# A fused convolution and two-layer MLP: another order of the first loads, taps without a detour, and wider VectorE calls

## The chip, the cores and the metric

The kernel runs on one core of one Trainium2 chip. The metric is the device time of one execution in microseconds. It is given as the median of several runs; the profile comes from one profiled execution.

## The reference

The input x has 8 sequences of 4096 tokens with 192 features, in float32. Eight heads of 24 features each have seven weights. A causal depthwise convolution comes first, and a two-layer MLP with exact GELU follows.

```python
w = exp(weight - max(weight)); w = w / (sum(w) + 1e-9)      # softmax over the 7 taps of a head
a[b, s, h, :] = sum_k w[h, k] * x_pad[b, s + k, h, :]        # 6 zeros ahead of each sequence
out = gelu(a.reshape(32768, 192) @ w_in) @ w_out             # w_in 192 x 2048, w_out 2048 x 192
```

The output is 32768 x 192 in float32.

## The kernel before

**Layout.** The tokens are cut in two halves of 16384. The two halves lie side by side on the 128 partitions, 64 features of each. The 192 features make three such thirds, `p` = 0, 1, 2 (`NP` = 3). A block `n` takes `WS[n]` tokens of each half: blocks 0 to 5 have 256, all later ones 512.

**Stages of a block.** `load` brings x to `xin` in four DMAs. `trans` (L529) transposes 32x32 squares on VectorE into `xT`. The seven taps follow: one `tensor_scalar` (L555) and six `scalar_tensor_tensor` (L562) for each third, into `acc` and at last `xc` in bf16. `mm1` (L763) multiplies a slice of W_in (`win`) with `xc` into `hp`. ScalarE takes the GELU of the slice into `gT` (L684). `mm2` (L793), or `mm2_t` (L823) for the 512-token blocks, multiplies with W_out and is interleaved with the next block's `mm1`. The results go through `osb` to memory. A slice `(n, i)` is one GELU call; a 256-token block has 8 slices, a 512-token block 16.

**The first two blocks** (`PC`) take their convolution on TensorE. `pconv` (L714) multiplies `xTb`, a bf16 copy of `xT`, with seven diagonal matrices `dg` into PSUM `ob`, and `conv_out` (L191, L193) copies the result to `xc`. Each third is a "kind" in a bank of its own; the last third is cut in two kinds of 128 tokens. The second half kind of the last third is computed crosswise (`ex` = 1), so that it can run in other quadrants of the array beside another kind. Block 0 is loaded in an order of its own: 8 neighbouring tokens in one partition, as runs of 5760 bytes that also hold features that are not used. Its history (`halo`) then takes copies on GpSimd (L417).

**The taps' weights.** The softmax runs on 8 partitions (`wsb`, `wex`, `wrc`), and five transposes (L485, L488) spread the result to all 128 partitions as `wcol`.

**W_in and W_out.** GpSimd's queue carries W_in with a cast to bf16, each half of the partitions getting one half of the columns. `FP` cuts that into a quarter, a quarter and a half (`S_WIN[0..2]`). `dup` on VectorE (L505) copies each piece to the other half of the partitions. SyncE loads W_out in four calls, and GpSimd casts it (L460).

**Order.** Everything is written out by hand: each engine has one list of instructions, and semaphores tie the lists together. The lists that matter here are

- SyncE: `wsb`, half of block 0's x, a wait for `S_WIN[0]`, block 1's x, W_out, x of blocks 2 and 3.
- GpSimd: W_in piece 0, the diagonal mask `idb`, W_in pieces 1 and 2, history of block 0, the bf16 copy of block 1, the casts of W_out.
- VectorE: the softmax, `dg`, `trans` of block 0, `conv_out`, `dup(0)`, `dup(1)`, `trans` of block 1, `dup(2)`, `conv_out` of block 1, then blocks 2, 3, ... with the copies out of PSUM at fixed places (`side`).
- ScalarE: half of block 0's x, the exponential, the casts of block 0, its share of `conv_out`, then the GELUs. For blocks 4 to 6 (`K0`) it also takes the first tap (L657).
- TensorE: 16 matmuls on zeros (L698, "warm"), `pconv` of block 0, then per slice `mm1` and a share of the previous block's `mm2`. The `pconv` of block 1 stands behind slices (0,4) and (0,5).

```python
            share = {1: [4, 12, 8, 8, 8, 8, 8, 8]}     # units of block 0's mm2 behind block 1's slices
                    wait_pc(t, n, NP - 2)              # mm1 of blocks 0, 1: xc's first two thirds
```

Of the kernel before, what the change touches and what calls it, by code (L numbers as in the profile page):

```python
# [11 lines left out]
def bass_lightweight_conv__then__act_gelu_exact_kernel(  # L12
# [16 lines left out]
    TB = 512  # L29
# [23 lines left out]
    HL = 32 * HB  # L53
    XB = HL + WS[0]
# [32 lines left out]
    CH = [[(8 * hf + i) % NF for i in range(NF)] for hf in range(2)]  # L87
# [3 lines left out]
    for n in range(NB):  # L91
        k = 64 if n == 0 or M0 <= n < M1 else 16 * NG[n] if n < NB - 1 else 32 * NG[n]
        OUTS.append(k * (NG[0] if n == 0 else 1) + (OUTS[n - 2] if n >= 2 else 0))
# [15 lines left out]
    with es:  # L109
        win = sbt("win", [128, NP * F], BF16)  # L110
        wout = sbt("wout", [128, NF * C], BF16)
        wsb = sbt("wsb", [H, KS], F32)
        wmx = sbt("wmx", [H, 1], F32)
        wsm = sbt("wsm", [H, 1], F32)
        wrc = sbt("wrc", [H, 1], F32)
        wex = sbt("wex", [H, KS], F32)
        wnm = sbt("wnm", [32, 32], F32)
        wnt = sbt("wnt", [32, 32], F32)
# [20 lines left out]
        S_XIN = [sem("S_XIN%d" % i) for i in range(NX)]  # L139
        S_OUT = [sem("S_OUT%d" % i) for i in range(2)]  # L140
# [32 lines left out]
        def kinds(n):  # L173
            w = WS[n]
            return [(0, 0, 0, w), (1, 1, 0, w), (2, 0, 0, w // 2), (2, 1, w // 2, w // 2)]


        PIECES = [(0, None), (1, 0), (1, 1), (2, None), (3, 0), (3, 1)]

        PA = (0, 2, 3, 5)  # L180

        def conv_out(e, n, j):
            kd, h = PIECES[j]
            p, ex, c0, w = kinds(n)[kd]
            e.wait_ge(S_PC, 4 * PC[n] + kd + 1)
            ro = slice(0, 128) if h is None else slice(64 * h, 64 * h + 64)
            ri = ro if not ex else slice(64 - 64 * h, 128 - 64 * h)
            dst = xc[n % 2][ro, p * TB + c0 : p * TB + c0 + w]
            src = bank(kd, ri, w)
# [5 lines left out]
        def wait_pc(e, n, p):  # L195

            if n == 0:
                e.wait_ge(S_PCA, (1, 2, 4)[p])
                if p >= 1:
                    e.wait_ge(S_PCE, p)  # L200
            else:
                e.wait_ge(S_PCE, 2 + (1, 3, 6)[p])

        NCV = NP * KS
        FQ = F // 8
        FH = F // 2
        FP = [0, FQ, 2 * FQ, FH]

        WG = [0, 4, 2, 6]

        def cast(e, n, p):
            e.wait_ge(S_TR, NP * n + p + 1)
            e.tensor_copy(
                ap(xTb[PC[n]], p * XB + HX, [[NP * XB, 128], [1, WS[n]]]),
                ap(xT[n % 2], p * XW + HX, [[NP * XW, 128], [1, WS[n]]]),
            ).then_inc(S_CAST[PC[n]])

        def cvd(n):

            return sum(NCV - NP * (m in K0) for m in range(n + 1) if m not in PC)  # L220


        HC = [0]
        for n in range(NB):
            HC.append(HC[n] + (1 + NP if n == 0 else 1))
# [5 lines left out]
        def xin_at(n):  # L231

            return 64 * (n // NX + 1)
# [85 lines left out]
        def load(e, n, qs=(0, 2, 1, 3), sm=None):  # L319
            mb = WS[n] // 32  # L320
            if n >= NX:
                e.wait_ge(S_TR, NP * (n - NX + 1))
            for q in qs:
                off = ((q // 2) * HALF + OFF[n]) * D + DQ * (q % 2)
                if n == 0:

                    dst = [[TB // 32 * DQ, 32], [1, mb * D - DQ]]
                    src = [[mb * D, 32], [1, mb * D - DQ]]
                else:
                    dst = [[TB // 32 * DQ, 32], [DQ, mb], [1, DQ]]  # L330
                    src = [[D, 32], [32 * D, mb], [1, DQ]]
# [4 lines left out]
        def store(e, m):  # L336
            if m < M0:
                for g in range(NG[m]):
                    wait_ev(e, m, g)
                    if m > 0:  # L340

                        e.dma_start(
                            ap(
                                outt,
                                (OFF[m] + 128 * g) * C,
                                [[C, 128], [HALF * C, 2], [1, C]],
                            ),
                            ap(osb[m % 2], g * C, [[8 * C, 128], [4 * C, 2], [1, C]]),
                        ).then_inc(S_OUT[m % 2], 16)
                        continue  # L350
                    mb = WS[m] // 32
                    for q in range(4):

                        e.dma_start(
                            ap(
                                outt,
                                (OFF[m] + 4 * g + q) * C,
                                [[mb * C, 32], [HALF * C, 2], [1, C]],
                            ),
                            ap(  # L360
                                osb[m % 2],
                                32 * q * 8 * C + g * C,
                                [[8 * C, 32], [4 * C, 2], [1, C]],
                            ),
                        ).then_inc(S_OUT[m % 2], 16)
# [18 lines left out]
        def _(g):  # L384
            def win_in(c0, c1, sm):
                for hf in range(2):
# [3 lines left out]
                    ).then_inc(sm, 16)  # L390

            win_in(FP[0], FP[1], S_WIN[0])
# [12 lines left out]
            for i in range(1, 3):  # L405
                win_in(FP[i], FP[i + 1], S_WIN[i])

            def halo(n):
                if n == 0:

                    t = xTb[0]
                    g.memset(
                        ap(t, 0, [[NP * XB, 128], [XB, NP], [32, HB]]), 0.0
                    ).then_inc(S_HALO)
                    for p in range(NP):
                        g.wait_ge(S_TR, p + 1)
# [502 lines left out]
```

## Time and profile before

| | us |
|---|---|
| median of 9 runs (682.05 to 684.11) | 682.68 |
| the profiled execution, device time | 683.04 |
| its span | 681.3 |
| PE (TensorE) busy | 674.8 (99%) |
| DVE (VectorE) busy | 561.8 (82%) |
| ACT (ScalarE) busy | 536.1 (79%) |
| POOL (GpSimd) busy | 38.9 (6%) |

PE is busy for nearly the whole span, so the time is what TensorE has to do, plus what it idles. In the profile a row such as `L763 PE MATMUL hp<-xc,win` names the line of the kernel, the engine, the operation and the tiles. The device time lies 1.74 us above the span. One matmul's record overlaps its neighbours', so the time of a stage is read from the starts of its first rows.

### The profile page before, as it was taken

The numbers are of one execution on the slowest core, as the hardware profiler recorded it, in microseconds if no ns is written. First come the engines' busy times: TensorE is split into PE (matmuls) and PEld (weight loads), VectorE is DVE, ScalarE is ACT, GpSimd is POOL, SyncE is SP. The second block draws the span as 40 slices with busy tenths as digits, with TensorE's granted clock in tenths as the row PEclk, the third lists the DMA queues.
The fourth block names the chain that finished last, engine by engine and source line by source line (L and its number), as shares of the span: only waits on it lengthen the run. The fifth ranks groups of instructions, "written<-read, shape, count | busy, mean of one in ns | idle before, by whom it ended". The sixth has DMA issues, their size and how long they took to land.

```text
span 681.3 us, 27316 instructions
## 1 busy us (share of the span) xinstructions
PE 674.8 (99%) x12576; PEld 410.6 (60%) x12576; DVE 561.8 (82%) x906; ACT 536.1 (79%) x548; POOL 38.9 (6%) x57
## 2 busy tenths in 40 slices
PE   8999999999999999999999999999999999999998
PEld 4899755555555555555555555555555555555557
DVE  6899989888889888898888898888898888988611
ACT  6899988777787777787877788777778777778772
POOL 5126100000000000000000000000000000000000
PEclk9999999999999999999999999999999999999999
DMA  9445333133442243432244322334322444311123
GB/s 224 81 105 130 72 71 75 42 76 95 96 93 56 45 93 94 95 78 49 65 95 94 94 65 46 82 94 96 92 51 49 95 94 96 74 45 26 48 50 94
DMA packets 132994, 54.79 MB, mean 80 GB/s; under 512 B 126480, under 2 KB 132752, under 8 KB 132880
## 3 DMA queue, kind: packets, MB, share of 16 engines
q1 hardware_dynamic: 130960, 51.50, 32.3%
q8 instruction: 98, 1.61, 1.0%
q0 software_dynamic: 1248, 0.79, 0.9%
q10 hardware_dynamic: 672, 0.76, 0.4%
q14 instruction: 16, 0.13, 0.1%
HBM read 28.66 MB, written 25.17 MB: 79 GB/s over the span
## 4 chain that ended last, share of the span: by engine, by line
PE 95%; DMA 2%; DVE 1%; SPq 1%; issue 0%; POOL 0%; POOLq 0%
PE hp L763 47%; PE ob L823 43%; PE ob L793 5%; DMA xin<-in_x_dram 1%; DVE acc L562 1%; PE hp L793 1%; DMA win<-in_moe_w_in_dram 1%; SPq L332 1%; SPq L877 0%; DVE xT L529 0%; POOL win L387 0%; DVE acc L555 0%; DVE xc L562 0%; DVE osb L283 0%; POOLq L904 0%
## 5 line engine op out<-in xcount | busy, mean ns | idle before, releaser
L684 ACT ACTIVATE gT<-hp 128x1024 bf16<-128x1024 f32 x512 | 522.7, 1023 | 129.9 <-PE hp L763 126.6
L763 PE MATMUL hp<-xc,win 64*64 64x512 bf16 (+2 forms) x6048 | 419.3, 366 | 2.4 <-ACT gT L684 1.1
L823 PE MATMUL ob<-gT,wout 64*64 64x512 bf16 x5376 | 366.3, 376 | 0.0
L562 DVE SCALAR_TENSOR_TENSOR acc<-xT,wcol,acc 128x512 f32<-128x512 f32 (+1 forms) x495 | 314.4, 699 | 0.0
L763 PEld LDWEIGHTS hp<-xc,win 64*64 64x64 bf16 (+1 forms) x6048 | 189.9, 106 | 135.2 <-ACT gT L684 3.3
L823 PEld LDWEIGHTS ob<-gT,wout 64*64 64x64 bf16 x5376 | 172.1, 118 | 123.0
L314 DVE STREAM_TRANSPOSE osb<-ob 128x512 f32<-128x512 f32 x84 | 74.2, 886 | 99.8 <-PE ob L823 99.8
L529 DVE STREAM_TRANSPOSE xT<-xin 128x512 f32<-128x512 f32 (+1 forms) x105 | 78.6, 796 | 4.2 <-DMA xin<-in_x_dram 4.2
L562 DVE SCALAR_TENSOR_TENSOR xc<-xT,wcol,acc 128x512 bf16<-128x512 f32 (+1 forms) x99 | 65.1, 712 | 0.0
L450 POOL COPY xT<-xT 128x18 f32<-128x18 f32 x30 | 27.9, 929 | 504.9 <-DVE xT L529 482.6
L793 PE MATMUL ob<-wout,gT 64*128 64x192 bf16 x896 | 47.6, 243 | 0.0
L793 PEld LDWEIGHTS ob<-wout,gT 64*128 64x128 bf16 x896 | 40.1, 94 | 3.9 <-issue 0.4
L555 DVE TENSOR_SCALAR acc<-xT,wcol 128x512 f32<-128x512 f32 (+1 forms) x90 | 37.6, 473 | 1.1
L698 PE MATMUL hp<-warm 128*128 128x512 bf16 x16 | 6.1, 562 | 1.3 <-DVE warm L466 1.3
L285 ACT ACTIVATE osb<-ob 128x192 f32<-128x192 f32 x2 | 0.7, 330 | 7.1 <-PE ob L793 7.1
L793 PE MATMUL hp<-wout,gT 64*128 64x192 bf16 x128 | 5.9, 243 | 0.0
L283 DVE COPY osb<-ob 128x192 f32<-128x192 f32 x2 | 0.7, 358 | 6.1 <-PE ob L793 6.1
L793 PEld LDWEIGHTS hp<-wout,gT 64*128 64x128 bf16 x128 | 5.3, 94 | 0.0
L657 ACT ACTIVATE acc<-xT,wcol 128x256 f32<-128x256 f32 (+1 forms) x9 | 5.2, 575 | 0.0
L698 PEld LDWEIGHTS hp<-warm 128*128 128x128 bf16 x16 | 2.1, 136 | 4.7 <-issue 3.2
L270 ACT ACTIVATE osb<-ob 128x384 f32<-128x384 f32 x10 | 4.9, 486 | 0.0
L387 POOL DMA_DIRECT2D win<-in_moe_w_in_dram x6 | 3.9, 658 | 0.8 <-POOLq L904 0.8
(36 smaller groups left out, 30.7 us busy)
## 6 DMA issues: line engine op xcount, KB each, us to landing
out_dram<-osb SPq DMA_DIRECT2D x122, 192.0 KB, 3.1
xin<-in_x_dram SPq DMA_DIRECT2D x116, 192.0 KB, 4.1
xin<-in_x_dram SPq DMA_DIRECT2D x20, 96.0 KB, 3.7
woutf<-in_moe_w_out_dram SPq DMA_DIRECT2D x4, 384.0 KB, 6.2
win<-in_moe_w_in_dram POOLq DMA_DIRECT2D x4, 96.0 KB, 4.3
win<-in_moe_w_in_dram POOLq DMA_DIRECT2D x2, 192.0 KB, 4.9
out_dram<-osb SPq DMA_DIRECT2D x8, 48.0 KB, 1.9
out_dram<-osb ACTq DMA_DIRECT2D x4, 96.0 KB, 2.0
```

The source lines that it names most:

```text
L314: v.transpose(ap(osb[m % 2], j, [[8 * C, 128], [C // 2, TB // 32], [NP, 32]]), bank(ring(m, j)),).then_inc(S_EV)
L332: e.dma_start(ap(xin[n % NX], 32 * q * (TB // 32 * DQ), dst), ap(xt, off, src)).then_inc(sm or S_XIN[n % NX], 16)
L450: g.tensor_copy(dst, src).then_inc(S_HALO)
L529: v.transpose(ap(xT[n % 2], p * XW + HX, [[NP * XW, 128], [1, w]]), ap(xin[n % NX], p, [[TB // 32 * DQ, 128], [D if n == 0 else DQ, w // 3 ...
L555: ins = v.tensor_scalar(a, src, wk, None, ALU.mult)
L562: ins = v.scalar_tensor_tensor(dst, src, wk, a, op0=ALU.mult, op1=ALU.add)
L657: a.activation(out=acc[n % 2][:, p * TB : p * TB + w], in_=ap(xT[n % 2], p * XW + HX, [[NP * XW, 128], [1, w]]), func=AF.Copy, scale=wcol[ ...
L684: a.activation(out=ap(gT[n % 2], i * c * 2 * w, dst), in_=ap(hp[u % 2], 0, src), func=AF.Gelu,).then_inc(S_GELU)
L698: t.matmul(hp[1][:, 0:512], warm[:, 0:128], warm[:, :])
L763: ins = t.matmul(hp[u % 2][fo : fo + fw, o : o + w], ap(win, f1, [[NP * F, 64], [2, fw]]), xc[n % 2][r, p * TB : p * TB + w], start=(p == ...
L793: ins = t.matmul(bb[sub], gT[m % 2][r, c0 : c0 + 128], wout[r, CH[sub][i] * C : (CH[sub][i] + 1) * C], start=(ph == 0 and i == 0), stop=(p ...
L823: ins = t.matmul(bank(ring(m, j), slice(64 * h, 64 * h + 64), w), ap(wout, 64 * hf * NF * C + CH[h][i] * C + j, [[NF * C, 64], [NP, 64]],) ...
```

## The change

Seven edits are made together:

1. Block 0's x is loaded like every other block's, in runs of 384 bytes. Its history is a memset on VectorE, and GpSimd's copies for it go.
2. GpSimd's queue carries, after the mask, the first half of each W_in half, then block 1's x (with its own semaphore `S_XP`), then the second half. `dup` has two steps and `CH` another order of the column chunks, so that slices (0,0), (0,1) need the first half, (0,2), (0,3) its copy, (0,4), (0,5) the second half and (0,6), (0,7) its copy. W_out comes in another grouping to match, and `UO` orders block 0's `mm2`.
3. SyncE waits for `S_WIN[1]` before W_out, and loads x of block 2 ahead of W_out's last part.
4. The softmax runs on all 128 partitions; two DMAs bring the weights there. The five transposes go.
5. The last third of block 0 is computed straight in both of its kinds, and `conv_out` copies it in two calls in place of three. `mm1` of slice (0,0) takes the last third after both chunks of the others.
6. Taps come in two calls (two thirds, one third) in place of three, `trans` in one call from block 2 on; the places in `side` are counted anew. `mm1` of a block waits for two thirds first.
7. Ten warm matmuls in place of 16; `pconv` of block 1 begins behind slice (0,3); `share` changes.

```diff
-    CH = [[(8 * hf + i) % NF for i in range(NF)] for hf in range(2)]
+    CH = [[(8 * hf + 8 * (i // 4 % 2) + 4 * (i // 8) + i % 4) % NF for i in range(NF)] for hf in range(2)]
...
-        PA = (0, 2, 3, 5)
+        PA = (0, 2, 3)
+        PV = (1, 4)
...
-        FP = [0, FQ, 2 * FQ, FH]
+        FP = [0, FH // 2, FH]
...
-                if n == 0:
-                    dst = [[TB // 32 * DQ, 32], [1, mb * D - DQ]]
-                    src = [[mb * D, 32], [1, mb * D - DQ]]
-                else:
-                    dst = [[TB // 32 * DQ, 32], [DQ, mb], [1, DQ]]
-                    src = [[D, 32], [32 * D, mb], [1, DQ]]
+                dst = [[TB // 32 * DQ, 32], [DQ, mb], [1, DQ]]
+                src = [[D, 32], [32 * D, mb], [1, DQ]]
...
-            win_in(FP[0], FP[1], S_WIN[0])
             g.wait_ge(S_MSET, 1)
...
-            for i in range(1, 3):
-                win_in(FP[i], FP[i + 1], S_WIN[i])
+            win_in(FP[0], FP[1], [S_WIN[0]] * 2)
+            load(g, 1, sm=S_XP)
+            win_in(FP[1], FP[2], S_WIN[1:])
...
-            halo(0)
             halo(1)
             for p in range(NP):
                 cast(g, 1, p)
-            for i in range(4):
+            halo(2)
+            for k in range(4):
...
-            v.memset(wnm[:, :], 0.0).then_inc(S_MSET)
-            v.wait_ge(S_WSB, 16)
+            v.memset(ap(xTb[0], HF, [[NP * XB, 128], [XB, NP], [1, HB]]), 0.0).then_inc(S_HALO)
+            v.wait_ge(S_WSB, 32)
...
-            v.transpose(wnt[:, :], wnm[:, :]).then_inc(S_PRO)
-            v.wait_ge(S_PRO, 5)
-            for q in range(4):
-                v.transpose(
-                    wcol[32 * q : 32 * q + 32, :],
-                    ap(wnt, 4 * (q % 2), [[32, 32], [1, 4], [0, 8]]),
-                ).then_inc(S_PRO)
...
-                ops = [] if n in K0 else [("t", n, p) for p in range(NP)]
-                ops += [("c", n, k, p) for k in range(int(n in K0), KS) for p in range(NP)]
+                ops = [] if n in K0 else [("t", n, 0)]
+                ops += [("c", n, k, q) for k in range(int(n in K0), KS) for q in range(2)]
                 if n + 1 in K0:
-                    ops[9:9] = [("t", n + 1, p) for p in range(NP)]
+                    ops[6:6] = [("t", n + 1, 0)]
...
             dup(0)
-            dup(1)
             for p in range(NP):
                 trans(1, p)
-            dup(2)
+            dup(1)
...
-                for j, at in enumerate([(n + 2, 18), (n + 3, 6), (n + 3, 9)]):
+                for j, at in enumerate([(n + 2, 12), (n + 3, 4), (n + 3, 6)]):
...
-            for i in range(16):
+            for i in range(10):
                 t.matmul(hp[1][:, 0:512], warm[:, 0:128], warm[:, :])
...
-            order = [0] * 4 + [1, 0] * 3 + [1, 2] * 4 + [3, 2] * 3 + [3] * 4
-            for kd in order:
+            for kd in [0] * 4 + [1, 0] * 3 + [1, 2, 2] * 3 + [1, 2] + [3] * 7:
                 pconv(*seq[kd].pop(0))
...
-                (0, 4): [(1, kd, k) for k in taps for kd in (0, 1)],
+                (0, 3): [(1, kd, k) for k in taps if k > 3 for kd in (0, 1)],
+                (0, 4): [(1, kd, k) for k in taps if k <= 3 for kd in (0, 1)],
...
-                        t.wait_ge(S_CV, cvd(n))
+                        t.wait_ge(S_CV, cvd(n) - 1)
...
-            share = {1: [4, 12, 8, 8, 8, 8, 8, 8]}
+            share = {1: [4, 4, 4, 10, 10, 10, 11, 11]}
...
-            sp.wait_ge(S_WIN[0], 32)
-            load(sp, 1)
-            for i in range(4):
-                g = WG[i]
-                sp.dma_start(
-                    ap(woutf, 2 * g * C, [[NF * C, 128], [2 * C, 2], [1, 2 * C]]),
-                    ap(woutt, 256 * g * C, [[2 * C, 128], [256 * C, 2], [1, 2 * C]]),
-                ).then_inc(S_WOUT[i], 16)
+            def wout_in(k):
+                sp.dma_start(
+                    ap(woutf, 2 * k * C, [[NF * C, 128], [8 * C, 2], [1, 2 * C]]),
+                    ap(woutt, 256 * k * C, [[2 * C, 128], [1024 * C, 2], [1, 2 * C]]),
+                ).then_inc(S_WOUT[k], 16)
+
+            sp.wait_ge(S_WIN[1], 16)
+            for k in range(3):
+                wout_in(k)
             load(sp, 2)
+            wout_in(3)
             load(sp, 3)
```

## The prediction

> **What bounds the kernel now.** I read the page first, then the stretches of time, the chain of waits, and the timeline of the first 30 us. The stretches (span, busy us of PE, PEld, DVE, ACT and POOL with counts, granted clock, DMA share, GB/s):
>
> ```profile
> 7.24:9.07 1.83, 1.54 (x57) 1.38 (x57) 0.74 (x3) 1.34 (x5) 0.60 (x3) 1.00 1.10 163
> 9.07:18.23 9.16, 7.75 (x152) 5.16 (x152) 7.20 (x16) 7.52 (x10) 4.01 (x6) 1.00 1.13 283
> 18.23:29.59 11.36, 10.69 (x224) 9.93 (x225) 9.49 (x25) 9.56 (x11) 1.28 (x3) 1.00 0.38 77
> 29.59:71.86 42.27, 42.27 (x898) 42.17 (x900) 42.23 (x90) 37.64 (x49) 16.59 (x4) 1.00 0.45 105
> 71.86:667.78 595.92, 595.92 (x10978) 339.39 (x10976) 495.22 (x754) 474.06 (x466) 11.11 (x27) 1.00 0.31 74
> ```
>
> From 29.59 us, when block 2's `mm1` starts, TensorE has no idle time at all until the last block's end. So the time is the moment of that start plus a fixed rest, unless VectorE falls behind; between 29.59 and 71.86 it is busy 42.23 of 42.27 us. Up to 29.59 TensorE starts late (7.24) and idles 2.37 us. The timeline tells what started when (start, us, engine, line, idle time before and its releaser):
>
> ```profile
> 5.92 0.15 PEld L698 LDWEIGHTS hp<-warm 128*128 128x128 bf16 x1 [0.28 <-issue]
> 6.00 1.34 DVE L529 STREAM_TRANSPOSE xT<-xin 128x256 f32<-128x256 f32 x3 [0.75 <-DMA xin<-in_x_dram]
> 6.29 0.53 PEld L698 LDWEIGHTS hp<-warm 128*128 128x128 bf16 x3 [0.21 <-issue]
> 7.24 1.54 PE L714 MATMUL ob<-xTb,dg 64*64 64x256 bf16 x56
> 9.67 1.27 PE L763 MATMUL hp<-xc,win 64*128 64x256 bf16 x20 [0.20 <-ACT xc L191]
> 10.32 4.92 ACT L684 ACTIVATE gT<-hp 128x1024 bf16<-128x1024 f32 x5 [0.71 <-PE hp L763]
> 18.23 0.83 PE L763 MATMUL hp<-xc,win 64*128 64x256 bf16 x12 [0.45 <-ACT gT L684]
> 20.06 1.34 DVE L529 STREAM_TRANSPOSE xT<-xin 128x256 f32<-128x256 f32 x3 [1.90 <-DMA xin<-in_x_dram]
> 29.59 0.83 PE L763 MATMUL hp<-xc,win 64*128 64x256 bf16 x12 [0.66 <-DVE xc L562]
> ```
>
> Two paths meet at 29.59. One goes from block 0's x (6.00) over `pconv` (7.24) and the first GELU (10.32) through TensorE's own work. The other goes from block 2's x (20.06) through its taps, and ended last by 0.66 us. The chain shows where that x was held up:
>
> ```profile
> 2.08 4.75 DMA win<-in_moe_w_in_dram
> 6.85 0.33 SPq L332
> 12.96 7.08 DMA xin<-in_x_dram
> 20.06 1.36 DVE xT L529 x3
> ```
>
> SyncE waited for W_in's first piece, issued block 1's x and all of W_out, and only then block 2's x, which took 7.08 us to land. So both paths must shorten for the time to fall.
>
> **Block 0's x.** It is 184 KB in each of four DMAs now and 96 KB after. Loads of the new kind, alone on the queues at 32 us, against W_in's, from issue to landing (min/median/max; the first line is x at 32 to 37 us, the second W_in):
>
> ```profile
> DMA to landing us min/median/max: 2.2/2.3/2.4
> DMA to landing us min/median/max: 3.6/4.7/5.1
> ```
>
> ScalarE issues its two at 0.87 and 1.30. SyncE's come one issue later than now, because a second DMA for the tap weights goes ahead (issue to issue 0.43): the last at about 2.12. With 2.3 the data is there at 4.45; with the 4.3 that the slowest of block 0's loads took now, at 6.4. I take 4.5, since W_in, the competitor, starts later too.
>
> The Trainium skill speaks against it: "DMA: Bandwidth & Descriptors", Specifications, wants transfers of at least 512 bytes, below which the engine reads, modifies and writes. By that rule 384-byte runs are slow; if each cost double, the landing would be 2.3 later and, as an estimate, the sum 682.7.
>
> The rows give 0.52 MB on SyncE's queue at 44.6% of 16 engines over 4.7 us (32.3 to 37), 15.5 bytes per ns and engine, and 0.37 MB on ScalarE's with 5760-byte packets at 37.2% over 4 us (1 to 5), also 15.5: a byte costs the same in both. I go by the rows, and the sum stays as below.
>
> **The taps.** The weights land 0.43 later (2.61 for 2.18). Reduce to `wcol` without the transposes took 1.25 (2.18 to 3.43), so 3.86, and `dg` takes 0.62: VectorE is free at 4.5, with the x. ScalarE's second table load shifts to 4.54, still ahead of the casts. `trans` starts at 4.55 for 6.00, `pconv` 1.24 later as now, at 5.8. The history copies that go had been hidden behind the casts; with the memset, block 0's stores are also 2 DMAs for 8 (27.11 to 32.6 on SyncE now), which only brings block 5's x sooner. The mask first and W_in after it costs GpSimd 0.64 (1.95 for 1.31).
>
> **`pconv` and the first GELU.** In units of 256 columns both orders make 14.5, so 1.54 stays. Now the last third of `xc` is out 2.43 after `pconv` starts (9.67); after, ScalarE has three copies (0.383, 0.375, 0.277) and VectorE one of 64x256 and one of 128x128 (0.424, 0.292), so it is out about 2.1 after, at 7.9, and two thirds of slice (0,0) are done by then. W_in's first half is issued at 1.95 and 2.65 and lands by the row above at 6.25 to 7.75, so it is just hidden; each 0.1 beyond costs 0.1. First GELU 8.75 for 10.32.
>
> **From there to block 2.** TensorE's work in this stretch is 7 slices and `pconv` of block 1 (7 x 0.66 + 0.96 + 0.59), then block 1's 8 slices and 64 units (16 x 0.66): 16.7 us. Now it takes 29.59 - 10.32 = 19.27, so it idles 2.6. Of this 0.66 is block 2's wait, and 1.2 came from block 1's x (landed 12.4) with `dup(2)` behind it until 15.83. After, GpSimd issues block 1's x at 3.3 to 5.9 and the second half by 7.2 (0.65 a call); W_in's packets ran from 4.8 to 9.7 beside x, some 2.1 us a half, and 1.7 us for x, put x at 9 and the second half at 10.5 to 11.4. GpSimd's own casts of x come after its DMA issues (done by 7.2), so no one waits for those; its `halo(2)`, now ahead of W_out's casts, waits for `trans` at 11.2, before W_out is there. VectorE then runs `dup(0)` 7.9 to 9.9 (2 x 0.98), `trans` to 11.2, `dup(1)` to 13.2, `conv_out` of block 1 to 15.6. Slice (0,2) needs `dup(0)` just when its GELU buffer comes free (9.8), (0,6) needs `dup(1)` at 14. ScalarE at 0.98 a GELU paces block 0, so some idling stays: with 1.5 for 2.6, block 2 can start at 8.75 + 16.7 + 1.5 = 26.95. Ends: 0.9 and 2.6, so 26.3 to 28.0.
>
> **Block 2's x.** SyncE, with W_out queued behind its wait for `S_WIN[1]`, resumes near 10 for 6.83. Ahead of x stand three W_out parts (their packet records show 123 of 1536 bytes in 0.5 us, so 1.04 for the 256 of a part), so x lands near 17, at worst as now relative to the first W_out issue (8.70 to 20.04), less one part and block 1's x: 10 + 11.3 - 1.0 - 1.7 = 18.6. `trans` in one call and two-call taps: 256 elements took 0.401, 512 took 0.667, so 0.135 is fixed per call; 1.07 a tap for 1.20, and 1.17 for `trans`, 0.72 for the first tap: 8.3 for 9.4, two thirds 0.4 earlier. Block 2 is ready at 24.9 to 26.5, ahead of TensorE. W_out's last part comes after x; its cast is done near 19, and slice (1,3) wants it near 20 because `share` puts only 12 units before; its cover is about 1 us, and a stall beyond costs one for one.
>
> **The rest.** One tap's call less per block saves VectorE about 1.1 us in 20.7, but there it waits 99.8 us for TensorE at L314 anyway: nothing. `trans` of blocks 4 to 6 now ends before ScalarE's first tap of all thirds instead of one; with block 2's x at 17 it ends 0.7 before it is wanted, so nothing, and 0.2 to 0.5 if x is late.
>
> **Sum.** 29.59 - 26.95 = 2.6; I take off 0.3 for the thin covers (`dup`, W_out, first taps): 2.3. The profiled 683.04 becomes 680.7; the median of the runs is 0.36 lower, so 680.4.
>
> **Rivals.** *The clock stays low.* Warm matmuls are 0.43 apart until 5.92 and then 0.2: the rate doubles near 6.2, though the granted clock reads 1.00 throughout. Ten of them end at 5.5, so `pconv` starts after a gap of 0.3 and before the rise. If the rise is only put off past `pconv` and the first slice, they take up to 1.54 + 0.3 more; of 2.3 is left 0.5 or a little more: 682.1. For it: the gap. Against it: 4.3 us of work is still ahead. The skill's "TensorE: Matmul & The Clock Gate", Part 1, says that about 3.4 us of sustained work in a free-running window raises the rate; by it a window that catches the gap could pass unraised, and the next is 3.4 us off; the sum by it is this rival's.
>
> *Block 0's x is no earlier* (lands near 6): only the 0.66 and part of the idling are won, 1.0: 681.7.
>
> *Slower: GpSimd's ring is the bottleneck.* 1024 runs of 384 bytes stand ahead of W_in's second half, and SyncE's wait hangs W_out and block 2's x on that half. Block 2's x lands 7 to 8.6 after `S_WIN[1]`, and block 2 starts 7.9 later. The time exceeds the old one once that half lands after 13 to 14.5, for 10 to 10.5 in the forecast: if each x call in the ring costs 0.65 + 1 us and more. At 1.6 more it lands at 16.5, block 2 starts near 32: 685.0. For it: no row shows small x runs in that ring. Against it: W_in's 192 packets a call cost 0.62 to 0.78 to issue and its 512-byte packet records read 60 ns each.
>
> **How the numbers follow.** Forecast 0.68 (679.4 to 681.8), clock 0.09, x no earlier 0.07, ring 0.16. A difference of 0.2% (1.37 us) is about what a measurement of this kernel can tell. Of the forecast 0.63 is faster; its upper end (0.05) and the two middle cases are no change. The range goes from full idling removed (26.3, no deduction: 679.4, rounded down) to 683.3, leaving out most of the ring case.
>
> **What would show it.** Right: block 0's first `trans` near 4.6, `pconv` near 5.8, first GELU near 8.75, block 2's `mm1` near 27 with no idle time after. Wrong: `pconv` lasting 2.5 us or more (clock), `trans` of block 0 near 6, block 1's x after 11 (ring), or idle TensorE at slices (1,3), (2,0) or (3,0).

## The result and the profile after

The changed kernel takes 685.55 us (median of 9 runs, 685.39 to 687.91), where the kernel before took 682.80 beside it (29 runs): a ratio of 1.0046, 95% interval 1.0038 to 1.0055. It is slower by about 0.46%, where 680.4 and faster was forecast, and outside the range of 679.2 to 683.3. The profiled executions show the same difference, 683.5 us of span for 681.3.

The stretches of the changed kernel, cut at the events that the prediction named. The columns are the stretch, its length, busy time of PE, PEld, DVE, ACT and POOL with counts, the granted clock, the DMA share and GB/s:

```profile
0.00:5.64 5.64, 4.38 (x10) 1.35 (x10) 1.09 (x8) 2.56 (x5) 4.42 (x13) 1.00 0.53 76
5.64:8.88 3.24, 0.01 (x1) 0.00 (x0) 1.69 (x4) 1.27 (x4) 1.17 (x2) 1.00 1.11 237
8.88:12.00 3.12, 3.12 (x56) 2.79 (x56) 0.67 (x2) 1.73 (x5) 0.20 (x1) 0.50 0.84 135
12.00:12.99 0.99, 0.99 (x18) 0.81 (x18) 0.84 (x2) 0.00 (x0) 0.00 (x0) 0.86 0.84 296
12.99:20.76 7.77, 6.77 (x141) 4.40 (x138) 6.49 (x14) 7.00 (x8) 4.15 (x7) 1.00 1.15 274
20.76:31.77 11.01, 10.88 (x224) 9.80 (x226) 10.94 (x20) 8.99 (x10) 1.49 (x3) 1.00 0.22 49
...
74.05:669.97 595.92, 595.92 (x10978) 338.81 (x10976) 465.96 (x503) 474.10 (x466) 16.88 (x27) 1.00 0.32 74
```

Read the last line first. The steady state lasts 595.92 us, to the hundredth what it lasted before (71.86 to 667.78). Block 2's first `mm1` starts at 31.77 for 29.59, 2.18 later, and the span is 2.2 longer: all of the loss lies ahead of block 2. Then read the second and third lines. TensorE does nothing from 5.64 to 8.88, and then runs `pconv`, 56 matmuls as before, at half the granted clock: 3.19 us (next view), where it took 1.54. In the fourth line the clock comes back: a mean of 0.86 over 0.99 us puts the step from 0.50 to 1.00 at 12.28.

The chain of waits of the changed kernel in the first 13 us (start, length, what) shows why TensorE had nothing to do:

```profile
0.81 0.77 SPq L833
...
1.64 0.61 SPq L833
...
2.30 0.44 SPq L337
2.74 0.05 issue
2.79 4.98 DMA xin<-in_x_dram
7.77 0.02 issue
7.80 0.53 DVE xT L491
...
8.41 0.43 ACT xTb L223
...
8.88 3.19 PE ob L665 x47
12.08 0.89 PE hp L723 x12
```

SyncE's two DMAs for the tap weights (L833) take 0.77 and 0.61 us to issue, where one took 0.40. They stand ahead of SyncE's half of block 0's x, whose last DMA is issued at 2.79 and lands 4.98 us later, at 7.77. Before, the last of that x had landed at 5.98.

The timeline of the changed kernel (start, busy, engine, line, operation; in brackets the idle time before it and its releaser) puts the other named events beside the forecast:

```profile
1.83 1.43 POOL L374 DMA_DIRECT2D win<-in_moe_w_in_dram  x2
...
4.29 0.16 DVE L428 TENSOR_REDUCE wmx<-wsb 128x1 f32<-128x7 f32 x1 [2.99 <-DMA wsb<-in_weight_dram]
...
7.80 1.32 DVE L491 STREAM_TRANSPOSE xT<-xin 128x256 f32<-128x256 f32 x3 [1.55 <-DMA xin<-in_x_dram]
...
12.99 3.89 ACT L635 ACTIVATE gT<-hp 128x1024 bf16<-128x1024 f32 x4 [1.03 <-PE hp L723]
...
19.96 1.22 DVE L491 STREAM_TRANSPOSE xT<-xin 128x768 f32<-128x768 f32 x1
...
21.54 0.85 POOL L418 CAST wout<-woutf 128x768 bf16<-128x768 f32 x1 [2.90 <-DMA woutf<-in_moe_w_out_dram]
...
31.77 0.82 PE L723 MATMUL hp<-xc,win 64*128 64x256 bf16 x12
```

The tap weights are there at 4.29 (forecast 2.61), block 0's first `trans` starts at 7.80 (4.55), the first GELU at 12.99 (8.75), block 2's x is transposed at 19.96 (landing near 17), the last cast of W_out starts at 21.54 (done near 19), block 2 starts at 31.77 (26.95), with no wait of TensorE just ahead of it.

### The profile page after: what moved, and what is told of

Its sections match the earlier page's. It is cut to its first block, busy times and chain, and to the rows that moved or that the text cites. A ratio compares the mean times of both kernels' runs of the same rounds, so it can differ in the third digit from the quotient of the medians.

```text
span 683.5 us, 26989 instructions
## 1 busy us (share of the span) xinstructions
PE 675.0 (99%) x12570; PEld 408.2 (60%) x12570; DVE 527.6 (77%) x605; ACT 535.9 (78%) x547; POOL 30.5 (4%) x55
## 4 chain that ended last, share of the span: by engine, by line
PE 98%; DMA 1%; ACT 0%; SPq 0%; DVE 0%; issue 0%; ACTq 0%
PE hp L723 48%; PE ob L784 42%; PE ob L754 5%; PE hp L754 1%; DMA xin<-in_x_dram 1%; PE ob L665 1%; ACT gT L635 0%; SPq L833 0%; DVE xT L491 0%; SPq L337 0%; ACT xTb L223 0%; DVE osb L293 0%; ACTq L219 0%
## 5 line engine op out<-in xcount | busy, mean ns | idle before, releaser
L519 DVE SCALAR_TENSOR_TENSOR acc<-xT,wcol,acc 128x1024 f32<-128x1024 f32 (+1 forms) x330 | 296.3, 954 | 5.3 <-ACT acc L608 5.3
L723 PEld LDWEIGHTS hp<-xc,win 64*64 64x64 bf16 (+1 forms) x6048 | 187.6, 106 | 135.3 <-ACT gT L635 2.2
L491 DVE STREAM_TRANSPOSE xT<-xin 128x1536 f32<-128x1536 f32 (+2 forms) x39 | 74.8, 1927 | 1.6 <-DMA xin<-in_x_dram 1.5
L519 DVE SCALAR_TENSOR_TENSOR xc<-xT,wcol,acc 128x1024 bf16<-128x1024 f32 (+1 forms) x66 | 60.7, 962 | 0.0
L408 POOL COPY xT<-xT 128x18 f32<-128x18 f32 x30 | 19.6, 654 | 511.8 <-DVE xT L491 483.6
L512 DVE TENSOR_SCALAR acc<-xT,wcol 128x512 f32<-128x512 f32 (+2 forms) x60 | 34.2, 613 | 1.1
L665 PE MATMUL ob<-xTb,dg 64*64 64x256 bf16 (+1 forms) x112 | 4.9, 305 | 3.2 <-ACT xTb L223 3.2
L665 PEld LDWEIGHTS ob<-xTb,dg 64*64 64x64 bf16 x112 | 3.8, 134 | 4.9 <-ACT xTb L223 4.1
L200 DVE CAST xc<-ob 64x256 bf16<-64x256 f32 (+3 forms) x8 | 2.9, 357 | 3.7 <-PE ob L665 3.5
L649 PE MATMUL hp<-warm 128*128 128x512 bf16 x10 | 4.4, 625 | 1.3 <-DVE warm L424 1.3
```

The costliest lines, as they stand in the source:

```text
L408: g.tensor_copy(dst, src).then_inc(S_HALO)
L491: v.transpose(out, src).then_inc(S_TR)
L512: ins = v.tensor_scalar(a, src, wk, None, ALU.mult)
L519: ins = v.scalar_tensor_tensor(dst, src, wk, a, op0=ALU.mult, op1=ALU.add)
L649: t.matmul(hp[1][:, 0:512], warm[:, 0:128], warm[:, :])
L665: ins = t.matmul(bank(kd, slice(64 * ho, 64 * ho + 64), w), dg[r, d0 : d0 + 64], xTb[PC[n]][r, x0 : x0 + w], start=(k == KS - 1), stop=(k ...
```

## The experiments

The theory after the result had two parts that follow each other: block 0's x lands late, because it is issued later and then meets the transfers of GpSimd's queue (W_in, and block 1's x); and the idle time that this opens at TensorE keeps the clock low over `pconv`. The rivals were that the shorter warm-up alone lowers the clock, that something later in the opening (W_out, block 2's x) binds anyway, and that the softmax on 128 partitions has a price of its own. The medians of the kernel before differ by up to 0.5 us between groups of runs, so each result stands as a ratio to the kernel before, run with it. Line numbers shift by a few lines between the variants; the operations are the same.

### More warm matmuls in the changed kernel

```
-            for i in range(10):
+            for i in range(22):
```

> The changed kernel with 22 warm matmuls for 10, so that TensorE stays busy until about 8.4 us. Theory 1 (TensorE idles from 5.6 to 8.9 us, and its clock is low for pconv and the first slice): pconv takes 1.55 us for 3.19, the granted clock from 8.9 to 13 us reads 1.00 for 0.59, block 2's mm1 starts near 30.1 for 31.8, and the time is near 684.0 for 685.55. Rival (pconv is slow because its casts and history come slowly): pconv stays above 2.5 us and the time within 0.4 of 685.55.

Measured: 684.09 for 682.94, ratio 1.0015 (1.0007 to 1.0024). Its timeline:

```profile
8.74 1.74 PE L665 MATMUL ob<-xTb,dg 64*64 64x256 bf16 x56 [1.06 <-ACT xTb L223]
...
11.49 3.89 ACT L635 ACTIVATE gT<-hp 128x1024 bf16<-128x1024 f32 x4 [0.67 <-PE hp L723]
...
23.62 1.24 PE L754 MATMUL ob<-wout,gT 64*128 64x192 bf16 x20 [0.57 <-POOL wout L418]
```

`pconv` starts where it did, and takes 1.74 for 3.19. The granted clock in that stretch of this kernel:

```profile
8.74:10.48 1.74, 1.74 (x56) 1.52 (x56) 0.64 (x2) 1.42 (x4) 0.20 (x1) 1.00 1.14 189
```

1.00 for 0.50. So the low clock cost 1.45 us of `pconv`, and the runs are 1.46 us nearer (685.55 to 684.09). That the two agree so closely is in part chance, since the profiled executions differ by only 0.73. The first GELU comes 1.50 earlier; block 2, at 31.02, only 0.75 earlier in the profile: TensorE now waits 0.57 for the last cast of W_out, which ends at 23.56 in this profile and 22.39 in that of the changed kernel.

### GpSimd's loads (W_in, block 1's x) held back until block 0's x is there

```
+            g.wait_ge(S_XIN[0], 64)
             win_in(FP[0], FP[1], [S_WIN[0]] * 2)
```

> The changed kernel, but GpSimd issues W_in and block 1's x only when all of block 0's x has landed. SyncE still issues its half of block 0's x at 2.3 and 2.8 us. Theory 2 (W_in's packets on the same DMA engines slow the short runs of block 0's x): that half lands 2.3 us after issue, near 5.1 for 7.8, and block 0's first trans starts when the taps are done, near 6.3 for 7.8; W_in's first half then lands near 9.7 (4.7 after issue), the first GELU comes near 10.7 for 13.0, time 684 to 685. Rival (the short runs themselves are slow on SyncE's queue at the start): that half still lands 4 us or more after its issue, trans starts at 7 or later, W_in is later by 3 us, and the time is over 687.

Measured: 687.65 for 682.94, ratio 1.0063 (1.005 to 1.0076). The time lies where the rival had put it (over 687), but it holds more than the question; the landing of SyncE's two x DMAs says what was asked. From issue to landing (min/median/max), in the changed kernel:

```profile
DMA to landing us min/median/max: 4.6/4.8/5.0
```

and with GpSimd's loads held back:

```profile
DMA to landing us min/median/max: 2.4/2.4/2.4
```

The same two DMAs, issued at the same moments, take 2.4 us without GpSimd's loads beside them and 4.8 with them. That competition, and no slow x, is the second half of the delay. The run holds W_in and block 1's x back together, so it does not tell which of the two weighs more. The x is then there at 5.16, but the first `trans` waits until 6.18, for VectorE to finish the tap weights: later than the 6.00 of the kernel before. So even with a free queue the changed softmax would have set block 0's start. The time is longer for reasons that belong to the edit: W_in is issued 3.6 us later (5.46) and `mm1` waits 0.83 us for it, `pconv` again takes 3.07 after a gap of 1.55, and TensorE waits 1.69 for W_out.

### The softmax of the taps back on 8 partitions

```
-            for hf in range(2):
-                sp.dma_start(
-                    ap(wsb, 64 * hf * KS, [[KS, 64], [1, KS]]),
-                    ap(wt, 0, [[KS, H], [0, 8], [1, KS]]),
-                ).then_inc(S_WSB, 16)
+            sp.dma_start(wsb[:, :], ap(wt, 0, [[KS, H], [1, KS]])).then_inc(S_WSB, 16)
...
+            v.transpose(wnt[:, :], wnm[:, :]).then_inc(S_PRO)
+            for q in range(4):
+                v.transpose(
+                    wcol[32 * q : 32 * q + 32, :],
+                    ap(wnt, 4 * (q % 2), [[32, 32], [1, 4], [0, 8]]),
+                ).then_inc(S_PRO)
```

> The changed kernel with the softmax of the taps undone: one small DMA for the weights, 8 partitions, five transposes. Theory 3 (the two tap DMAs hold up SyncE's queue by 1.04 us, so that its half of block 0's x meets W_in's packets): SyncE issues x at 1.3 and 1.7 us, most of it moves before W_in's first packets at 3.3, and it lands near 4.3 to 5; dg is ready at 5.3 as in the kernel before, so trans starts near 5.4 for 7.8 and pconv near 6.6. Time near 683.5 if the clock still stays low through pconv, near 682 if the gap of 1 us is too short for that. Rival (W_in's packets alone hold x up, whenever it is issued): x lands 5 us after its issue, near 6.5, trans near 6.6, time near 684.5.

Measured: 683.51 for 682.94, ratio 1.0013 (1.0004 to 1.0022); the rest of the change is as it was. Its timeline:

```profile
5.17 1.33 DVE L503 STREAM_TRANSPOSE xT<-xin 128x256 f32<-128x256 f32 x3
...
6.24 1.74 PE L677 MATMUL ob<-xTb,dg 64*64 64x256 bf16 x56 [0.53 <-ACT xTb L225]
...
9.07 3.89 ACT L647 ACTIVATE gT<-hp 128x1024 bf16<-128x1024 f32 x4 [0.75 <-PE hp L735]
...
22.10 0.83 POOL L420 CAST wout<-woutf 128x768 bf16<-128x768 f32 x1 [2.60 <-DMA woutf<-in_moe_w_out_dram]
...
22.99 2.03 PE L766 MATMUL ob<-wout,gT 64*128 64x192 bf16 x20 [2.27 <-POOL wout L420]
24.81 1.49 PE L735 MATMUL hp<-xc,win 64*128 64x256 bf16 x12
```

Here is the opening that was forecast: block 0's x landed at 4.47 (4.5 forecast; SyncE's DMAs issued at 1.26 and 1.69 landed in 2.3 to 2.8), `pconv` runs at the full clock after ten warm matmuls and a gap of 0.53, and the first GELU starts at 9.07 (8.75), 3.92 before that of the changed kernel. So the softmax on 128 partitions cost the opening both its x and its clock. But only 2.0 of the 3.9 reach the runs. (They spread from 682.66 to 685.25, and the profiled execution is the slowest of them; in it block 2 starts at 31.81, no earlier than in the changed kernel.) The last two lines say where the rest went. TensorE waits 2.27 us for the last quarter of W_out, and the wait costs it the clock once more: the granted clock reads 0.50 from 22.76 to 26.18, and the two rows take 2.03 and 1.49 us, where the same matmuls take 1.24 and 0.82 at the full clock (the version with block 3's x held back, below). From the first row to the next slice's `mm1` that is 3.97 us for 2.56, so 1.41 on top of the wait. In the chain of waits of this kernel the transfer behind that cast is one line:

```profile
14.85 7.20 DMA woutf<-in_moe_w_out_dram
```

7.20 us from issue to landing, the longest of the four of W_out in this kernel, of which the shortest took 3.5. Unless another kernel is named, the remaining experiments start from this one.

### Fewer warm matmuls in the kernel before

```
-            for i in range(16):
+            for i in range(10):
```

> The kernel before with 10 warm matmuls for 16: that part of the change alone. Theory 1 (a gap ahead of pconv lowers or keeps low the clock): TensorE idles from 5.6 to 7.2, pconv takes 2.5 to 3.1 us for 1.54, the first GELU comes 1.0 to 1.6 later, of which block 2's start takes up part: time 683.3 to 684.4 for 682.8. Rival (4.3 us of warm work is enough): pconv stays at 1.5 to 1.7, and the time within 0.3 of 682.8.

Measured: 683.06 for 682.94, ratio 1.0001 (0.9992 to 1.0009). In the stretches of this kernel the clock falls during `pconv`, after a gap of 1.93, and stays down over the first slice:

```profile
7.09:9.50 2.41, 2.41 (x58) 2.19 (x60) 0.67 (x2) 1.73 (x5) 0.75 (x3) 0.66 1.10 175
9.50:11.04 1.54, 1.54 (x16) 0.94 (x18) 1.41 (x4) 0.27 (x1) 0.00 (x0) 0.50 1.15 252
```

The first GELU is 0.72 later, and the runs do not show it:

```profile
29.49 0.82 PE L763 MATMUL hp<-xc,win 64*128 64x256 bf16 x12
```

Block 2 starts at 29.49, for 29.59, and now without the 0.66 us that TensorE waited there for its `xc` in the kernel before: the loss went into that wait (block 2's x also came 0.3 earlier in this profile, at 19.74). So the shorter warm-up costs nothing there because the path through block 2's x is as late. In the changed kernel there is no such wait ahead of block 2, and the loss counts.

### Block 0's x ahead of the tap weights

In the changed kernel, with its softmax on 128 partitions:

```
+            load(sp, 0, (0, 1))
             for hf in range(2):
                 sp.dma_start(
                     ap(wsb, 64 * hf * KS, [[KS, 64], [1, KS]]),
                     ap(wt, 0, [[KS, H], [0, 8], [1, KS]]),
                 ).then_inc(S_WSB, 16)
-            load(sp, 0, (0, 1))
```

> The changed kernel with SyncE's half of block 0's x ahead of the two tap DMAs. If only the place of x in SyncE's queue was at fault (theory 3 as first put): x lands near 4, the taps' reduce comes within 0.5 of where it was (4.3), dg ends near 6.8, trans starts there for 7.8, pconv near 8.0, time near 684.5. Rival (the tap weights for 128 partitions are a cost of their own, 2.5 us from issue to landing and meeting W_in's packets): the reduce comes 0.9 or more later, at 5.2 to 6.5, dg ends at 7.2 to 8.5, and the time stays at 685 to 686 although x is there at 4.

Measured: 686.58 for 683.14, ratio 1.0055 (1.0041 to 1.0069). Its timeline:

```profile
1.75 1.41 SPq L834 DMA_DIRECT2D wsb<-in_weight_dram  x2
...
7.30 0.16 DVE L428 TENSOR_REDUCE wmx<-wsb 128x1 f32<-128x7 f32 x1 [6.01 <-DMA wsb<-in_weight_dram]
...
9.18 1.31 DVE L491 STREAM_TRANSPOSE xT<-xin 128x256 f32<-128x256 f32 x3
...
10.25 3.20 PE L665 MATMUL ob<-xTb,dg 64*64 64x256 bf16 x56 [4.55 <-ACT xTb L223]
```

The x lands at 4.29, and waits for the taps: their second DMA, issued at 2.56, lands 4.7 us later, against 2.6 in the changed kernel, where it was issued at 1.64. The reduce at 7.30 comes later than even the rival had it (5.2 to 6.5). `dg` is done at 9.26. So the order of issue only chooses which of the two meets GpSimd's loads; the 128-partition load has a price in either place. The rival of a price of its own holds.

### W_out ahead of block 2's x, and block 3's x held back

Two ways to let W_out's last quarter through. The first issues it ahead of block 2's x:

```
-            for k in range(3):
+            for k in range(4):
                 wout_in(k)
             load(sp, 2)
-            wout_in(3)
```

> The kernel with the taps' softmax undone (block 0 reaches its first GELU at 9.1 us there, but TensorE waits 2.3 us for W_out's last cast near 23, and block 2 starts at 31.8), and now with all four W_out parts ahead of block 2's x, as in the kernel before. Theory 4 (the order of SyncE's queue decides what is late): W_out's last cast ends near 19, no wait for it; block 2's x lands 1 us later, near 21, so block 2 starts near 29.0 and the time is near 682.2. Rival (the transfers are slow together, whatever their order): the W_out wait goes, but block 2's x lands at 22 or later, block 2 starts at 30 or later, time 683 or more.

Measured: 681.97 for 682.68, ratio 0.9994 (0.9981 to 1.0007). The wait for W_out is gone, block 2's x is transposed at 20.23, block 2 starts at 28.37. The runs spread from 681.29 to 686.15, so this ratio alone does not tell it from no change.

The second leaves the order and makes the x of block 3, and so of block 4, wait:

```
             wout_in(3)
+            sp.wait_ge(S_XIN[2], 64)
+            sp.wait_ge(S_WOUT[3], 16)
             load(sp, 3)
```

> The kernel with the taps' softmax undone, and SyncE issuing block 3's x (and all behind it) only when block 2's x and W_out's last part have landed. Theory 5 (block 3's and 4's x, wanted only near 29 us, share the engines and hold up the two that are wanted now): block 2's x lands near 18 for 20.5, W_out's last part near 19 for 22.0, TensorE's wait for W_out falls to under 0.5, block 2 starts near 28.3 for 31.8, and the time is near 680.5 to 681.5. Rival (short runs of x and W_out rows are slow by themselves): both land within 0.7 of where they did, time unchanged near 683.5, or later for block 3's x.

Measured: 681.87 for 682.68, ratio 0.9985 (0.9976 to 0.9993). Its timeline:

```profile
19.11 1.24 DVE L503 STREAM_TRANSPOSE xT<-xin 128x768 f32<-128x768 f32 x1 [3.19 <-DMA xin<-in_x_dram]
...
20.78 1.24 PE L766 MATMUL ob<-wout,gT 64*128 64x192 bf16 x20 [0.24 <-POOL wout L420]
21.86 0.82 PE L735 MATMUL hp<-xc,win 64*128 64x256 bf16 x12
...
28.18 0.82 PE L735 MATMUL hp<-xc,win 64*128 64x256 bf16 x12
```

Nothing is sent earlier here; two loads that stand behind are sent later. Block 2's x is transposed 1.4 earlier than with the 8-partition softmax alone (20.49), the wait for W_out falls from 2.27 to 0.24, and block 2 starts 3.6 earlier, of which 1.4 is the clock that no longer falls. W_out's last quarter landed 4.9 us after its issue, for 7.2. One profile of each could mislead, since these times vary. But in the five profiles with this order of issue and no deferral (the changed kernel, the three of its variants above, the 8-partition softmax) that quarter took 6.5 to 8.2 us, and in the three with this deferral and nothing else changed on SyncE 4.9, 5.8 and 6.0; and the ratio to the kernel before falls from 1.0013 to 0.9985. So the x of the next blocks, issued after these two on the same queue, had held them up. The first edit removes the wait by another way, and its block 2's x is nearly as late as without it.

Both together:

```
-            for k in range(3):
+            for k in range(4):
                 wout_in(k)
             load(sp, 2)
-            wout_in(3)
+            sp.wait_ge(S_XIN[2], 64)
             load(sp, 3)
```

> Both of the last two edits: W_out's four parts, then block 2's x, then a wait for that x before block 3's. If theories 4 and 5 both hold: W_out's last cast ends near 18.5, block 2's x lands near 18.5, block 2 starts near 27.9 to 28.3, time near 680.3 to 681. If only the order matters it equals the first of these runs, if only the sharing, the second.

Measured: 682.05 for 682.68, ratio 0.9989 (0.998 to 0.9997). Block 2's x is transposed at 21.32 and block 2 waits 0.57 for its `xc`; TensorE still waits 0.45 for a W_out cast. Together they are no better than one, where 680.3 to 681 was expected. In this profile, 0.9 us above the median of its kernel, block 2's x is the late one; why it came no earlier with W_out ahead of it is not shown.

The deferral alone, in the kernel before:

```
+            sp.wait_ge(S_XIN[2], 64)
             load(sp, 3)
```

> The kernel before, with SyncE issuing block 3's x only when block 2's x has landed. Theory 5 (block 3's x slows block 2's): block 2's first trans at 18.5 to 19.3 for 20.06, the 0.66 us of idling ahead of block 2 goes, time near 682.2 for 682.9. Rival: block 2's x lands within 0.3 of 20, the time stays.

Measured: 682.55 for 682.68, ratio 0.9997 (0.9988 to 1.0006). In the profile block 2's x is earlier (19.34 for 20.06) and block 2 starts at 28.89 for 29.59, but the medians differ by 0.13, which these runs can't tell from nothing. A gain of the deferral shows in the runs only where block 0 has been brought forward.

### What still binds, and a version that beats both

On top of the deferral, two more warm matmuls, to see whether any clock was left to win:

```
-            for i in range(10):
+            for i in range(12):
```

> The fastest kernel so far (taps' softmax undone, block 3's x held back) with 12 warm matmuls for 10, so that the gap ahead of pconv falls from 0.5 us to none. If the clock is low in part of the executions there (pconv 2.2 in one profile of its sister, 1.74 in the others): pconv 1.55 to 1.75, time 681.2 to 681.7 with less spread, for 681.87. If not: the same within 0.2.

Measured: 682.73 for 683.14, ratio 0.9989 (0.998 to 0.9998). `pconv` takes 1.74, as it did in the profile without the two, and the ratio is no lower, so none shows. In this profile the last cast of W_out came at 21.23 in spite of the deferral, and TensorE waited 1.47: the cover was still too thin for an unlucky execution.

SyncE waiting for W_in's first half in place of its second, so that W_out starts earlier:

```
-            sp.wait_ge(S_WIN[1], 16)
+            sp.wait_ge(S_WIN[0], 32)
```

> The fastest kernel so far (taps' softmax undone, block 3's x held back), with SyncE waiting for W_in's first half in place of its second before W_out, as the kernel before waits for the first piece. Theory 6 (what is left of TensorE's wait at slice (1,3) comes from W_out starting 2.2 us later than it could): W_out's parts are issued from 8.2 us, its last part lands near 18 for 19.8, the wait for its cast goes, W_in's second half lands up to 1 us later (11.5 to 12.5) and is still in time for slice (0,4); block 2 starts near 27.8, time near 681.4 with less spread. Rival (the engines are full, and what starts earlier only takes from W_in's second half): slices (0,4) to (0,7) wait 1 us or more for it, and the time is 682 or more.

Measured: 681.55 for 683.0, ratio 0.9982 (0.9973 to 0.999). W_out's last cast is done at 20.35 and nobody waits for it, but W_in's second half now lands at 12.96, and TensorE waits for that:

```profile
13.09 0.83 PE L735 MATMUL hp<-xc,win 64*128 64x256 bf16 x12 [0.83 <-DMA win<-in_moe_w_in_dram]
```

One short wait is traded for another. Instead of moving the transfer, the last version moves the work that needs it:

```
-            share = {1: [4, 4, 4, 10, 10, 10, 11, 11]}
+            share = {1: [4, 4, 4, 0, 13, 13, 13, 13]}
```

> The fastest kernel so far with block 0's mm2 units shared out as 4, 4, 4, 0, 13, 13, 13, 13, so that W_out's last part is wanted one slice later. Theory 6, other side: the wait for W_out's last cast (0.2 to 1.5 us in the profiles) falls by up to 1.0 and slice (1,3) idles 0.3, so 681.4 to 681.8 with less spread. Rival (block 2's x is late in the same executions, so the gain is lost at block 2): the same within 0.2.

Measured: 681.55 for 683.0, ratio 0.998 (0.9971 to 0.9989). Its timeline:

```profile
18.85 1.23 DVE L503 STREAM_TRANSPOSE xT<-xin 128x768 f32<-128x768 f32 x1 [2.94 <-DMA xin<-in_x_dram]
...
20.76 0.83 POOL L420 CAST wout<-woutf 128x768 bf16<-128x768 f32 x1 [2.98 <-DMA woutf<-in_moe_w_out_dram]
...
28.39 0.82 PE L735 MATMUL hp<-xc,win 64*128 64x256 bf16 x12
```

The last cast ends at 21.59, and TensorE, done with its other work at 21.49, takes it up at 21.64; block 2 starts at 28.39 with no wait. W_out's last quarter still comes last here, by 0.15 us instead of 2.27. This is the changed kernel with the old softmax, the x of block 3 deferred, and no units of `mm2` at slice (1,3). It beats the kernel before by 0.2%, and by the two ratios (1.0046 over 0.998) the changed kernel by some 0.66%.

What stays open is why W_out's transfers vary: in the three profiles with the deferral and the same wait of SyncE, whose transfers up to there are the same, the third cast starts at 16.95, 17.06 and 18.13, and the runs of the version with W_out first spread over 4.9 us. No run here separates that.

## Why the prediction was wrong, step by step

Block 2 was forecast to start at 26.95 and started at 31.77, 4.82 later. That splits along the prediction's own steps: `pconv` starts 3.08 late (8.88 for 5.80), from there to the first GELU takes 1.16 more (4.11 for 2.95), and from the first GELU to block 2 0.58 more (18.78 for 18.2).

**Block 0's x, the step that failed first.** The prediction charged the second tap DMA as "one issue later", 0.43, from the spacing of other DMAs. The rows give 0.77 and 0.61 for two DMAs of 64 rows of 28 bytes, where one of 8 rows took 0.40. So SyncE's last x was issued at 2.79, not 2.12. Then came 4.98 to land, where 2.3 was taken from loads that were alone on the queues at 32 us. The row with the right condition stood beside it, 4.3 for block 0's own x under W_in, and was put aside with the sentence that W_in starts later too. W_in's first DMA was issued at 1.83, for 1.31 before, but x had moved by more. The run with GpSimd's loads held back shows that it is the company and not the short runs: 2.4 without it.

**The taps.** The weights were to land at 2.61 and `dg` to be done at 4.5. They landed at 4.26, the reduce started at 4.29, and VectorE was through at 6.25, a microsecond after the 5.25 of the kernel before. The rows of the kernel before had only the 8-row DMA, and the delay of its landing was carried over to two DMAs with sixteen times as many rows. This term alone would have put the first `trans` at 6.2, as the run with GpSimd's loads held back shows, so the forecast's 4.55 could not be had with these tap DMAs at all.

**The clock, a rival given 0.09.** It was right in size (up to 1.54 + 0.3 more; 1.45 measured on `pconv`) and in the gap as the cause, but it was priced by itself, with a gap of 0.3. The gap was 3.24, because x was late: "x no earlier" and "clock low" were two cases in the forecast, 0.07 and 0.09, and were one case on the chip. With x as early as forecast the clock was full, as the 8-partition run shows (1.74 after a gap of 0.53).

The way there was another than the rival's, which had the rise put off. In the trace of the changed kernel the records of the granted clock begin at 5.45, as the warm matmuls end; they read 1.00 up to 8.86, 0.50 up to 12.28, and 1.00 from there. So the clock had risen and fell again, 0.02 us ahead of `pconv`. (Ahead of its first record every profile reads 1.00, whatever the pace. In the kernel before the first record is at 6.21, where the warm matmuls double their pace, so I take it for the rise.) In the two other profiles with ten warm matmuls and a long gap, GpSimd's loads held back and block 0's x first, the records begin only at 10.05 and 13.33: there the rise was put off, and `pconv` took 3.07 and 3.20, much the same.

The skill page "TensorE: Matmul & The Clock Gate", Part 1, gives about 3.4 us of work for the clock to rise and an idle window of that length for it to fall. The length agrees: the steps above are 3.41 us apart, and so are those of the kernel before with ten warm matmuls (4.46, 7.87, 11.28). That the window must be idle throughout does not: the clock fell after 3.41 us of which TensorE had worked 0.20 (changed kernel), 1.48 (kernel before with ten) and 1.37 (8-partition softmax, 19.35 to 22.76). It stayed up over 1.79 (GpSimd's loads held back, 23.70 to 27.11). Counted in steps of 3.41 back from the first record, it rose after stretches with 2.80 of work or more, and had not risen after 2.49, 2.55 and 2.62. These are single profiles; no run was made to find the limits.

**From the first GELU to block 2.** 16.7 of work and 1.5 idle were forecast, 18.2. In the two stretches from 12.99 to 31.77 TensorE is busy 6.77 + 10.88 = 17.65 and idle 1.13. Read in the same way, the kernel before is busy 17.40 of its 19.27 and idle 1.87, not 2.6. So the work, summed from single rows of 0.66, was 0.95 too small, and there was less idling to remove: it fell by 0.74, and the path by 0.49 where 1.07 was forecast. In the best version, where block 0 starts early, this path takes 19.41, and nothing comes out of it.

**W_out and block 2's x.** "A cover of about 1 us" for W_out's last part, with the cast done near 19, and x landing near 17, worst 18.6. The cast ended at 22.39 in the changed kernel and at 22.93 with the 8-partition softmax; x was transposed at 19.96 and 20.49. The packet sum stopped at what stood ahead of them in the queue. The x of the blocks behind was left out, and it held both up: deferring it gave 1.4 on x and 2.0 on the wait in the first pair of profiles (x was transposed at 18.60 to 20.05 in the other three with it). In the changed kernel this failure cost nothing to be seen, since TensorE was late enough itself; with block 0 early it took about half of the gain, in part by a second fall of the clock.

**The ring rival (0.16, the slower side).** The sign was right for another reason. GpSimd's four x calls took 2.35 us (0.59 each, against the 0.65 of the forecast), W_in's second half let SyncE go at 10.5, forecast near 10, and W_out was not held by the ring. The ring hurt by what its first loads did to block 0's x.

**What held.** At the full clock the new order of `pconv` takes 1.74, not far from the 1.54 of the forecast, which counted it as unchanged. The steady state did not move at all, though VectorE's busy time in it fell from 495.22 to 465.96. In the waits of the changed kernel (engine, tile and line, releaser: us, times, longest) the time went where the prediction put it:

```profile
DVE osb L324 <- PE ob L784: 129.0, 30, 11.8
```

VectorE waited 99.8 us there before. And the opening did decide the whole: 2.18 us at block 2 became 2.2 of span. With the failed steps repaired one after another the forecast's sign comes back, at 681.55 for 683.0, and some 60% of its size: 1.45 of the 2.3.

## What to carry to other kernels

Take the duration of a transfer from a row in which the same neighbours were running, and count as neighbours the DMAs issued after it too: here both what stood behind in the same queue and what ran on another ring held a load up. A DMA of many tiny rows pays at its issue as well as at its landing, so spreading a small table over all partitions belongs behind the loads that the first matmul needs, or is done on chip. A stall of TensorE can also cost it the clock, at its first real work as later on, so the two are one case with one price, and warm matmuls are worth sizing to the latest landing rather than to the expected one.

## What was unexpected of the hardware

- Two DMAs that bring 28-byte rows to 64 partitions each took 0.77 and 0.61 us to issue on SyncE, and one that brings 8 such rows 0.40. The second landed 2.6 us after its issue when issued at 1.64, and 4.7 when issued at 2.56, beside W_in and block 1's x.
- SyncE's two DMAs of block 0's x, in runs of 384 bytes, landed in 2.4 us without GpSimd's loads and in 4.6 to 5.0 beside them: a factor of two from company alone.
- The granted clock fell to 0.50 within `pconv` after 1.93 us of idling, with ten warm matmuls ahead. It read 1.00, with 1.74 for `pconv`, after 0.53 (ten) and 1.06 (twenty-two). In the version with W_out first `pconv` took 2.20 after 0.54 (ten), at a clock that reads 1.00: the first record of that profile is at 7.23, inside `pconv` (6.25 to 8.45). So a reading of 1.00 ahead of a profile's first record does not show a full clock.
- Two `tensor_scalar` calls on VectorE took 1.32 us in the changed kernel at 21.22, while GpSimd's cast of W_out ran beside them from 21.54, and 0.75 at 30.06, with no cast. The skill page "SBUF — State Buffer", section "SBUF: two separate sides", says that VectorE, in some of its modes or with two inputs from SBUF, and GpSimd share a port pair that one of them holds for a whole instruction while the other waits. These rows agree with it, and the price moves with the cast. In the last version the cast starts at 20.76, after the two calls: they take 0.75, and the ten `scalar_tensor_tensor` beside it 5.97, for 5.37 in the changed kernel. With W_out first the cast is over at 19.60, and nothing is slow (0.77 and 5.37).
